# Alternating two PSUM banks in a feed-forward pass, and requesting the second-level weights two pairs ahead

## The chip, the cores and the metric

One core of a Trainium2 chip runs the whole program. The metric is the device time of one execution in microseconds. TensorE is called PE here, VectorE is DVE in the profile's rows, ScalarE ACT, GpSimd POOL; SP is the engine whose queue issues the transfers.

## The reference

A transformer block in float32 on 2048 tokens of width 1024, with modulation vectors taken from a condition `c`:

```python
h = _layernorm(x, axis=-1) * (1 + ca) + sa
x = x + ga * _A_ref(h, A_wq, A_wk, A_wv, A_wo, A_beta)   # 32 heads, 4 segments of 512 tokens with a memory
h = _layernorm(x, axis=-1) * (1 + cb) + sb
x = x + gb * _B_ref(h, B_w_gate, B_w_up, B_w_down)

def _B_ref(x, w_gate, w_up, w_down):                     # 1024 -> 3584 -> 1024
    return (_gelu(x @ w_gate) * (x @ w_up)) @ w_down
```

The change lies in the second half: the second layer norm and the gate and up products of `_B_ref`.

## The kernel before, in words

Every float32 operand is cut into a high and a low part (`cut`: ScalarE rounds the high part, VectorE or GpSimd subtracts to get the low one), and each product of a 128x128 tile is three matmuls: high x high, high x low, low x high. A matmul has 512 moving columns and fills one PSUM bank.

The program runs in stages. Attention and its projection (`project`, L753) come first; the projection works in `block(s, half)`, where s is a segment of 512 tokens. Each of the block's four tiles of 128 tokens takes 24 matmuls into a bank of a ring of two (`mm_ps`), is read out at L777 with the residual, and stored to `x1_d`. Beside it runs the second normalisation (`norm_tiles`): it loads a tile nb of `x1_d`, takes statistics (L235 to L241), scales (L246, L248), turns the tile with 8 transposes on PE (L269), applies the modulation (L275, L277) and stores to `h2_d`.

The feed-forward multiplies in Winograd's seven-product form of a 2x2 blocked product: the blocks of the left side are two token halves by two halves of the width, those of the right side are (gate, up) by the two halves of the width. Products are numbered 1 to 7. There are two groups of 1024 tokens, p = 0 and 1, and 28 chunks fc of 128 feature columns.

- The second-level stage, `two(n)` for n = 0 to 13 (L1087): products 1 and 2 of both token groups are split again in the seven-product form, over a pair of chunks. i = 1 and 2 are the two outer products. Per pair there are 14 products of 6 matmuls. The results go to `st_d`: the outer product 1 in the left half of a row, gelu of products 1 + 2 in the right half. The left sides AA stay in SBUF; `a_first` (L993) prepares them from `h2_d` while the projection ends (tiles u, cut into AA). The right sides BB of pair n + 1 are prepared beside pair n by `b_two` (L1045) from tiles g, loaded by `b_two_load` into a ring of four `raw` tiles, two to a pair. Pair 0 runs all of i = 1 and then all of i = 2; the others take turns.
- The passes, `gate_up(m)` for m = 0 to 55 (L1309): p = m // 28, and the other five products of a chunk, 12 matmuls each, go into two banks pb and pc (tiles f) out of a ring of five (`s_ps`). c1 and g1 are the two halves of the `st_d` row (`cg_load`), u2 and u3 sums in SBUF, g the pair of results that is stored to `hid_d`. In the first 28 passes `b_part(m + 1)` prepares the next chunk's weights B from `wg` and `wu` and stores them to `bc_d` and `bt_d`; in the second 28 they are read back (tiles B and ag), and `w_all` prepares the down weights beside (rw from `wd`, T, stored to `wc_d`). In the first passes `a_mix(1)` (L943) mixes the second token group (four steps, L959, whose inputs rm come by transfer), and in pass 23 `row_parts` makes the row gbb. `a_next(p)` (L1155) cuts the left sides A of a token group: twenty cuts, each into slots that the products before have left. That of group 0 runs beside pair 13, that of group 1 beside pass 27.
- The down product, `down()` (L1438), 2352 matmuls in another order of the seven.

What fixes the order: PE, VectorE, ScalarE and GpSimd run in the order in which the code is written, and from the second-level stage on SP too. Side work stands in generators on the list `sides`; `step()` (L799) advances each of them by its rate, and is called once after every product of a pair, twice per product in a pass, four times per tile of the projection. `later(k, f)` emits f k steps on; `flush` runs a side to its end.

A pass before, with the banks that the products use:

```python
product(pb, 6, True);  u2 = pb + c1            # L1335
product(pb, 7, False); u3 = pb + c1            # L1338, bank holds 6 + 7
product(pc, 5, True);  u3 = pc + u3            # L1341
product(pb, 4, False); h2 = gelu(pb + c1)      # L1346, L1347
product(pc, 3, False); u2 = pc + u2; h1 = g1 * u2; h2 = h2 * u3   # L1350 to L1352
```

Of the kernel before, what the change touches and what calls it, by code (L numbers as in the profile page):

```python
# [22 lines left out]
T = 2048  # L23
# [6 lines left out]
L = 512  # L30
# [6 lines left out]
def block_kernel(ctx: ExitStack, tc: tile.TileContext, x, c, wmod, wq, wkv, wo, beta, wg, wu, wd, out):  # L37
# [787 lines left out]
    def projections():  # L825
        def block(s, *nbs):
            for _ in project(s, [(i, nb) for i in range(4) for nb in nbs]):
                step()
                yield

        wsp = wsp_tile("xr")
        xrs.extend([[f32(wsp[:, a, b * L:(b + 1) * L]) for a in range(2) for b in range(2)], -1])
        cols = lambda s: [load_hT(oT_d, s, oh[s], f"o{s}", True), 1]
        ahead = load_hT(oT_d, 1, oh[1], "o1", True)
        sides.append([chain(islice(ahead, 1), iter([None] * 3), ahead), 1])
        two = [project(0, [(i, 0)]) for i in range(2)]
# [24 lines left out]
        ff["pools"](2)  # L861
        sides.append([ff["first"], 2])
        yield from block(3, 1)
        flush("n")
# [10 lines left out]
    PRODUCTS = (6, 7, 5, 4, 3)  # L875
# [4 lines left out]
    def feed_forward():  # L880
# [111 lines left out]

        def a_first():  # L993

            get = {1: [(raw_tile, raw_tile)] * 2, 2: [(ra_tile, ra_tile), (lambda n: pair_tile(n, "T", 5),) * 2]}
            ts = {}

            def load(i, c):
                ts[i, c] = [unit(i, c, p, get[i][c][p]) for p in range(2)]
# [3 lines left out]
            for c in range(2):  # L1003
                load(1, c)
            load(2, 0)
            for _ in range(3):
                yield
            for i in (1, 2):
                sums = {}
                if i == 2:  # L1010
                    while len(ffp) < 4:
                        yield
                    load(2, 1)
# [31 lines left out]
        def b_two(n):  # L1045
# [14 lines left out]
            yield from seven(b11, b12, b21, b22, t1, t2_, put, nc.vector, ROUND)  # L1060

        def seven(b11, b12, b21, b22, t1, t2_, put, eng, which):

            diff(t1, b12, b11)
            if 1 in which:
                put(1, b11, nc.vector)
                yield
# [5 lines left out]
            if 2 in which:  # L1073
                put(2, b21, nc.vector)
# [6 lines left out]
            put(5, t1, eng)  # L1081
# [3 lines left out]
            put(3, b22, eng)  # L1085

        def two(n):  # L1087
# [67 lines left out]
        def a_next(p):  # L1155
# [44 lines left out]
        def b_part(fc):  # L1200
# [23 lines left out]
            yield from seven(g[:, :L], u[:, :L], g[:, L:], u[:, L:], t1, t2_, put, nc.gpsimd, PRODUCTS)  # L1224
# [84 lines left out]
        def gate_up(m):  # L1309
# [23 lines left out]
            u2, u3 = (c_tile(f"c{q}_{m}") for q in range(2))  # L1333
            product(pb, 6, True)
            nc.vector.tensor_add(u2, pb, c1)  # L1335
# [5 lines left out]
            nc.vector.tensor_add(u3, pc, u3)  # L1341
            step()
            product(pb, 4, False)
            g = pair_tile(f"g{m}", "g", 3)
            h1, h2_ = (g[:, q] for q in range(2))
            nc.vector.tensor_add(h2_, pb, c1)  # L1346
            nc.scalar.activation(h2_, h2_, AF.Gelu_apprx_tanh)  # L1347
# [4 lines left out]
            nc.vector.tensor_mul(h2_, h2_, u3)  # L1352
# [194 lines left out]
        pools(3)  # L1547
        gbb = ffp[3].tile([P, D], F32, name="gbb")
        for n in range(NJ):
            if n == 1:  # L1550
                sides.append([chain(norm_tiles(x1_d, h2_d, (3,), 4, 3, "c", wait=6, get=ra_tile), wait_for(6), a_mix(0)), 1, "m"])
            if n + 1 < NJ:
                sides.append([b_two(n + 1), 1, "b"])
            else:
# [10 lines left out]
        cg_load(0)  # L1565
        for m in range(NCH):
            p, fc = divmod(m, FC)
            if m + 1 < FC:
                if m == 0:
                    gu_load(1)  # L1570
# [3 lines left out]
            if m + 1 < NCH:  # L1574
                cg_load(m + 1)
# [339 lines left out]
```

## Time and profile before

| what | us |
|---|---|
| median of 3 runs (lowest, highest) | 2900.39 (2898.39, 2905.28) |
| the profiled execution, its own time | 2895.0 |
| its span | 2893.3 |
| attention and projection | 0 to 1110 |
| second-level stage, 14 pairs | 1116 to 1450 |
| passes 0 to 27 | 1450 to 1897 |
| passes 28 to 55 | 1897 to 2356 |
| down product | 2356 to 2893 |

Times inside the trace are microseconds from the span's start. A timeline row gives start, length, engine, line, operation, output <- inputs, count, and in brackets the idle time before it with what ended it. In a view of waits a row reads: who waited <- for whom: total us, times, longest. A row by windows gives for each engine its busy time and instruction count, then the granted clock of PE (1.00 is full), the mean busy share of the 16 DMA engines and GB/s. Matmuls overlap: one takes 0.39 us from start to end, but the next starts earlier, so the end of a stretch lies later than the end of its last issue.

### The profile page before, as it was taken

The page shows a single profiled execution, that of the slowest core. Times are in us where ns is not written, and L with a number is a line of the kernel's source. Part 1 is how long each engine was busy: PE and PEld are TensorE (multiplying, and loading weights), DVE is VectorE, ACT ScalarE, POOL GpSimd, SP SyncE. Part 2 cuts the span into 40 slices and gives each one's busy share as a digit, 9 for nine tenths or more (in the row PEclk, how much of TensorE's full clock was granted, in tenths as well). Part 3 has the DMA queues.
Part 4 walks back from the last instruction along what each step waited for, and adds up shares of the span by engine and source line. Part 5 has one row for each costly group of instructions (what it writes and reads, how often), then busy time and mean ns, then how long its engine had stood idle before and what let it go on. Part 6 is the DMA issues. An engine that isn't in the chain of part 4 may idle for free.

```text
span 2893.3 us, 42626 instructions
## 1 busy us (share of the span) xinstructions
PE 2716.8 (94%) x14068; PEld 2233.6 (77%) x14068; DVE 1766.4 (61%) x3746; ACT 1260.1 (44%) x2924; POOL 1056.1 (37%) x1646
## 2 busy tenths in 40 slices
PE   7999999999999996998888999988888899999999
PEld 6888888888887885776666777767767778888887
DVE  7676658676677455666645555555656555475456
ACT  7787777766776333443422222221211233234322
POOL 3333335333335323555555666534646400000000
PEclk9999999999999998999999999989999999999999
DMA  6446446444435674565587766678988888696564
GB/s 248 134 141 164 110 126 167 118 125 130 130 114 165 213 245 132 180 210 200 195 297 280 268 245 246 230 261 304 324 298 323 301 302 273 236 308 230 174 195 140
DMA packets 266189, 613.38 MB, mean 212 GB/s; under 512 B 26992, under 2 KB 51568, under 8 KB 265968
## 3 DMA queue, kind: packets, MB, share of 16 engines
q1 hardware_dynamic: 265968, 610.66, 63.6%
q8 instruction: 111, 1.82, 0.3%
q14 instruction: 110, 0.90, 0.1%
HBM read 372.53 MB, written 187.70 MB: 194 GB/s over the span
## 4 chain that ended last, share of the span: by engine, by line
PE 73%; DVE 10%; DMA 8%; issue 4%; POOL 3%; ACT 2%; SPq 1%; DVEq 0%; POOLq 0%; ACTq 0%
PE y L1525 18%; PE f L1325 18%; PE kv L395 8%; PE q L401 6%; PE y L773 5%; PE S L607 3%; PE T L695 3%; PE O L707 3%; DMA g<-wg 2%; DVE BB L922 2%; PE kT L514 2%; PE vT L514 1%; DVE g L1352 1%; DVE c L1335 1%; PE pb L1106 1%
## 5 line engine op out<-in xcount | busy, mean ns | idle before, releaser
L1325 PE MATMUL f<-A,B 128*128 128x512 f32 x3360 | 802.3, 399 | 103.4 <-DVE c L1335 93.2
L1325 PEld LDWEIGHTS f<-A,B 128*128 128x128 f32 x3360 | 641.5, 192 | 263.8 <-DVE c L1335 63.9
L1525 PE MATMUL y<-B,L 128*128 128x512 f32 x2352 | 533.3, 389 | 0.0
L1525 PEld LDWEIGHTS y<-B,L 128*128 128x128 f32 x2352 | 441.4, 188 | 91.7
L611 ACT ACTIVATE sj<-sj,mm 128x384 f32<-128x384 f32 (+3 forms) x512 | 281.1, 552 | 40.1 <-DVE mm L609 39.5
L609 DVE CUSTOM_DVE_ANT_0 sj<-S,mask 128x384 f32<-128x384 f32 (+3 forms) x512 | 228.2, 488 | 97.8 <-PE S L607 70.8
L698 POOL TENSOR_SCALAR_AFFINE_SELECT pt<-pt 128x128 f32<-128x128 f32 x512 | 166.8, 347 | 331.1 <-ACT pt L697 323.1
L1347 ACT ACTIVATE g<-g 128x512 f32<-128x512 f32 x56 | 35.4, 632 | 514.9 <-DVE g L1346 503.5
L697 ACT ACTIVATE pt<-T 128x256 f32<-128x256 f32 (+3 forms) x512 | 182.3, 444 | 132.3 <-PE T L695 125.8
L925 ACT ACTIVATE L<-X 128x512 fp32r<-128x512 f32 x168 | 105.8, 630 | 260.0 <-PE y L1525 164.4
L922 DVE TENSOR_TENSOR L<-X,L 128x512 fp32r<-128x512 f32 x168 | 115.8, 690 | 147.7 <-ACT L L925 147.7
L386 POOL TENSOR_TENSOR w<-r,w 128x256 fp32r<-128x256 f32 x180 | 133.8, 774 | 141.7 <-ACT w L380 139.2
L1239 POOL TENSOR_TENSOR rw<-rw,gbb 128x256 f32<-128x256 f32 x112 | 103.2, 957 | 221.2 <-DMA rw<-wd 207.2
L395 PE MATMUL kv<-w,hha 128*128 128x256 f32 x896 | 175.2, 286 | 2.3 <-DVE vx L413 2.3
L1106 PE MATMUL pb<-AA,BB 128*128 128x512 f32 x504 | 132.3, 411 | 29.8 <-DVE x L1122 21.9
L395 PEld LDWEIGHTS kv<-w,hha 128*128 128x128 f32 x896 | 145.1, 192 | 3.4 <-DVE vx L413 2.5
L1106 PEld LDWEIGHTS pb<-AA,BB 128*128 128x128 f32 x504 | 97.3, 197 | 57.4 <-DVE x L1122 27.9
L395 PE MATMUL kv<-w,hla 128*128 128x256 f32 x448 | 127.3, 284 | 0.0
L773 PE MATMUL y<-wo,hho 128*128 128x512 f32 x384 | 126.5, 394 | 0.0
L925 ACT ACTIVATE B<-t 128x512 fp32r<-128x512 f32 x84 | 52.2, 621 | 147.6 <-POOL t L922 147.6
L695 PE MATMUL T<-qs,ks 128*128 128x256 f32 (+3 forms) x512 | 105.6, 327 | 1.8 <-DVE ry L674 1.1
L607 PE MATMUL S<-ks,qs 96*128 96x384 f32 (+3 forms) x512 | 106.9, 329 | 0.3
(283 smaller groups left out, 5184.5 us busy)
## 6 DMA issues: line engine op xcount, KB each, us to landing
B<-wc_d SPq DMA_DIRECT2D x112, 512.0 KB, 4.1
cg<-st_d SPq DMA_DIRECT2D x112, 256.0 KB, 5.3
hid_d<-g SPq DMA_DIRECT2D x56, 512.0 KB, 4.0
wc_d<-T SPq DMA_DIRECT2D x56, 512.0 KB, 5.3
X<-hid_d SPq DMA_DIRECT2D x112, 256.0 KB, 4.8
bc_d<-B SPq DMA_DIRECT2D x54, 512.0 KB, 5.4
B<-bc_d SPq DMA_DIRECT2D x54, 512.0 KB, 6.4
wr<-gd_d SPq DMA_DIRECT2D x84, 256.0 KB, 4.2
```

Of the source, the lines that this page charges most:

```text
L395: nc.tensor.matmul(ps, b[:, sl], w[:, a], start=(kt == 0 and a == 0 and b is hi), stop=(kt == KT - 1 and a == 1), **kw)
L401: nc.tensor.matmul(ps, w[:, a], b, start=(kt == 0 and a == 0 and b is hi), stop=(kt == KT - 1 and a == 1), **kw)
L607: nc.tensor.matmul(ps[:, :nk], qs[:96, j, i * P:(i + 1) * P], ks[:96, j, :nk], start=True, stop=True)
L609: nc.vector.tensor_tensor_reduce(out=sj[:, :nv], in0=ps[:, :nv], in1=mask[:, L - nv:], scale=-1.0, scalar=3.4e38, op0=ALU.add, op1=ALU.min ...
L611: nc.scalar.activation(sj[:, :nv], sj[:, :nv], AF.Exp, bias=mm[:, j, i:i + 1], scale=-1.0, accum_out=ll[:, i, j:j + 1])
L695: nc.tensor.matmul(ps[:, :nn], ks[:, j, kc * P:(kc + 1) * P], qs[:, j, L - nn:], start=True, stop=True)
L697: nc.scalar.activation(pt, ps[:, nn - n:nn], AF.Exp)
L773: nc.tensor.matmul(ps, b[:, i * P:(i + 1) * P], w[:, a, g % 2], start=(g == 0 and a == 0 and b is hi), stop=(g == G - 1 and a == 1))
L922: f(*xs)
L1106: nc.tensor.matmul(ps, w[:, a, at:at + P], A["a", i, r, k][b], start=(r in (1, 6, 5) and k == a == b == 0), stop=(k == 1 and a == 1), skip ...
L1325: nc.tensor.matmul(ps, B[m, i][:, a, kt * P:(kt + 1) * P], A[p, i, kt][b], start=(start and kt == 0 and a == 0 and b == 0), stop=(kt == 3 ...
L1525: nc.tensor.matmul(banks[t], ops[k][:, y, t * P:(t + 1) * P], B[slots[k]][:, x], start=(i not in (2, 4, 3) and j == 0 and x == 0 and y == ...
```

## The change

1. In a pass the products come in the order 6, 5, 7, 3, 4 (`PRODUCTS`), which puts them on the banks pb, pc, pb, pc, pb. u3 starts from product 5 and adds the bank of 6 + 7; the last multiplication of the second half is emitted two steps later. The weights for a pass are prepared in a matching order by a new function `five`, with the three differences first; `seven` keeps only the second-level stage.
2. `b_two_load(n + 2)` is called when pair n begins (before: n + 1). Pairs 1 and 2 are requested in pair 0 between its two halves, and the preparation of pair 1 begins there.
3. The first loads for the passes, `cg_load(0)`, `cg_load(1)` and `gu_load(1)`, move into pair 13, behind the last product that used the slots; `cg_load` then runs two passes ahead.
4. The normalisation of segment 2 in the projection's last blocks runs at rate 2 (before: 1).
5. In `a_first` both columns' sums are taken before the first cut, and the last tiles of i = 2 are requested as soon as their pool exists. In `a_next` the load of a further tile stands ahead of a cut instead of behind it.

```diff
-        sides.append([norm_tiles(x1_d, h2_d, (2,), 4, 3, "b", get=ff["ra"]), 1, "n"])
+        sides.append([norm_tiles(x1_d, h2_d, (2,), 4, 3, "b", get=ff["ra"]), 2, "n"])
...
-    PRODUCTS = (6, 7, 5, 4, 3)
+    PRODUCTS = (6, 5, 7, 3, 4)
...
                 for r in ROUND[1:] if i == 1 else ROUND:
-                    if (i, r) == (1, 2):
-                        continue
-                    for c in range(2):
-                        if r == 6:
+                    if r == 6:
+                        for c in range(2):
                             summed(c)
                             yield
+                    for c in range(2):
+                        if (i, r) == (1, 2):
+                            continue
...
+        def five(b11, b12, b21, b22, t1, t2_, put):
+
+            diff(t1, b12, b11)
+            yield
+            diff(t2_, b22, t1)
+            yield
+            diff(b12, b22, b12)
+            yield
+            put(6, t2_, nc.vector)
+            yield
+            put(5, t1, nc.gpsimd)
+            yield
+            put(7, b12, nc.vector)
+            diff(t2_, b21, t2_)
+            yield
+            put(3, b22, nc.gpsimd)
+            yield
+            yield
+            put(4, t2_, nc.vector)
...
                 product(i, r)
+                if n == 0 and (i, r) == (1, 3):
+                    for q in (1, 2):
+                        b_two_load(q)
+                    sides.append([chain(wait_for(1), b_two(1)), 1, "b"])
+                if n == NJ - 1 and (i, r) == (2, 4):
+                    for q in range(2):
+                        cg_load(q)
+                    gu_load(1)
                 ended(i, r)
...
             for q, (i, b) in enumerate(todo):
+                if q > 1:
+                    load()
...
                     put_a(p, i, 2 * b + k, rs[q][:, k], nc.vector)
-                    if k:
-                        load()
...
             product(pb, 6, True)
             nc.vector.tensor_add(u2, pb, c1)
             step()
+            product(pc, 5, True)
+            nc.vector.tensor_add(u3, pc, c1)
+            step()
             product(pb, 7, False)
-            nc.vector.tensor_add(u3, pb, c1)
-            step()
-            product(pc, 5, True)
-            nc.vector.tensor_add(u3, pc, u3)
-            step()
-            product(pb, 4, False)
...
+            nc.vector.tensor_add(u3, pb, u3)
             step()
             product(pc, 3, False)
             nc.vector.tensor_add(u2, pc, u2)
             nc.vector.tensor_mul(h1, g1, u2)
-            nc.vector.tensor_mul(h2_, h2_, u3)
+            step()
+            product(pb, 4, False)
+            nc.vector.tensor_add(h2_, pb, c1)
+            nc.scalar.activation(h2_, h2_, AF.Gelu_apprx_tanh)
+            later(2, lambda: nc.vector.tensor_mul(h2_, h2_, u3))
             step()
...
         pools(3)
+        units(2, 1)
...
-            if 0 < n < NJ - 1:
-                b_two_load(n + 1) if n + 1 not in two_raws else None
-            if n == NJ - 2:
+            if 0 < n < NJ - 2:
+                b_two_load(n + 2)
+            elif n == NJ - 2:
                 gu_load(0)
...
-            if m + 1 < NCH:
-                cg_load(m + 1)
+            if m + 2 < NCH:
+                cg_load(m + 2)
```

More of the change, by code (lines that the diff above doesn't have):

```diff
@@ L991, in a_early, with units @@
                     yield
+        get = {1: [(raw_tile, raw_tile)] * 2, 2: [(ra_tile, ra_tile), (lambda n: pair_tile(n, "T", 5),) * 2]}
+        ts = {}
+        def units(i, c):
+            ts[i, c] = [unit(i, c, p, get[i][c][p]) for p in range(2)]
         def a_first():
[L995 to L999, printed above, removed]
             while not normed(0, 2):
@@ L1003, in a_first @@
             for c in range(2):
-                load(1, c)
-            load(2, 0)
+                units(1, c)
+            units(2, 0)
             for _ in range(3):
@@ L1009, in a_first @@
                 sums = {}
[L1010 to L1013, printed above, removed]
+                while (i, 1) not in ts:
+                    yield
                 def summed(c):
@@ L1059, in b_two, with seven @@
             t1, t2_ = (tmp_tile(f"t{q}_a{n}").rearrange("p (i m) -> p i m", i=2) for q in (1, 2))
-            yield from seven(b11, b12, b21, b22, t1, t2_, put, nc.vector, ROUND)
-        def seven(b11, b12, b21, b22, t1, t2_, put, eng, which):
+            yield from seven(b11, b12, b21, b22, t1, t2_, put)
+        def seven(b11, b12, b21, b22, t1, t2_, put):
             diff(t1, b12, b11)
-            if 1 in which:
-                put(1, b11, nc.vector)
-                yield
+            put(1, b11, nc.vector)
+            yield
             diff(t2_, b22, t1)
@@ L1072, in seven @@
             yield
-            if 2 in which:
-                put(2, b21, nc.vector)
+            put(2, b21, nc.vector)
             diff(b12, b22, b12)
@@ L1080, in seven @@
             yield
-            put(5, t1, eng)
+            put(5, t1, nc.vector)
             yield
@@ L1084, in seven @@
             yield
-            put(3, b22, eng)
+            put(3, b22, nc.vector)
+        def five(b11, b12, b21, b22, t1, t2_, put):
[13 more added lines that the diff above has]
+            put(3, b22, nc.gpsimd)
+            yield
+            yield
+            put(4, t2_, nc.vector)
         def two(n):
@@ L1223, in b_part @@
                 t1, t2_ = (a_tile(48 + 2 * (fc % 2) + q, f"t{q}_{fc}", F32) for q in range(2))
-            yield from seven(g[:, :L], u[:, :L], g[:, L:], u[:, L:], t1, t2_, put, nc.gpsimd, PRODUCTS)
+            yield from five(g[:, :L], u[:, :L], g[:, L:], u[:, L:], t1, t2_, put)
         def w_all():
@@ L1333, in gate_up @@
             u2, u3 = (c_tile(f"c{q}_{m}") for q in range(2))
+            g = pair_tile(f"g{m}", "g", 3)
+            h1, h2_ = (g[:, q] for q in range(2))
             product(pb, 6, True)
@@ L1551, in feed_forward @@
                 sides.append([chain(norm_tiles(x1_d, h2_d, (3,), 4, 3, "c", wait=6, get=ra_tile), wait_for(6), a_mix(0)), 1, "m"])
-            if n + 1 < NJ:
+            if 0 < n < NJ - 1:
                 sides.append([b_two(n + 1), 1, "b"])
-            else:
+            elif n:
                 flush("m")
@@ L1564, in feed_forward @@
             flush("b")
-        cg_load(0)
         for m in range(NCH):
```

6 lines of the change are left out of this document (removed).

## The prediction

> **What bounds the kernel now.** I read the page first. Its chain that ended last is 73% PE, and among its groups these three carry the argument (busy us and mean ns of one, then idle time before them and its releaser):
>
> ```profile
> PE 73%; DVE 10%; DMA 8%; issue 4%; POOL 3%; ACT 2%; SPq 1%; DVEq 0%; POOLq 0%; ACTq 0%
> ...
> L1325 PE MATMUL f<-A,B 128*128 128x512 f32 x3360 | 802.3, 399 | 103.4 <-DVE c L1335 93.2
> ...
> L1525 PE MATMUL y<-B,L 128*128 128x512 f32 x2352 | 533.3, 389 | 0.0
> ```
>
> The last row gives PE's own pace, since nothing interrupts it: 533.3 / 2352 = 0.2267 us for a 128x512 matmul. A product of a pass (12 matmuls) is then 2.72 us, a pass (60) 13.60, 28 passes 380.9, a pair of the second-level stage (84) 19.05. The passes' 3360 matmuls would take 761.8 us; they are busy for 802.3 and stand idle for 103.4 more. Who ends PE's waits, from the view of waits, and then the stretches of the feed-forward (length; busy time and count of PE, PEld, DVE, ACT, POOL; clock; DMA share; GB/s): first pair, pair 1, pairs 2 to 12, pair 13, first 28 passes, second 28, down product.
>
> ```profile
> PE f L1325 <- DVE c L1335: 93.2, 56, 7.0
> ...
> PE pa L1106 <- ACT c L1116: 9.3, 8, 2.7
> PE f L1325 <- DVE c L1341: 9.1, 4, 2.8
> ...
> PE pa L1106 <- DVE xr L777: 6.2, 1, 6.2
> ```
> ```profile
> 1116.45:1160.62 44.17, 27.54 (x84) 20.57 (x85) 29.38 (x40) 15.91 (x27) 19.55 (x21) 0.74 0.33 113
> 1160.62:1180.02 19.40, 19.40 (x90) 16.07 (x88) 12.56 (x22) 10.14 (x17) 11.96 (x16) 1.00 0.32 109
> 1180.02:1418.90 238.88, 219.79 (x955) 174.40 (x954) 154.58 (x247) 96.90 (x173) 127.32 (x157) 1.00 0.60 201
> 1418.90:1450.27 31.37, 25.75 (x86) 19.02 (x85) 19.70 (x32) 16.50 (x30) 13.60 (x18) 0.78 0.66 214
> 1450.27:1897.40 447.13, 400.96 (x1697) 320.29 (x1695) 249.62 (x315) 108.77 (x188) 268.38 (x328) 0.98 0.74 263
> 1897.40:2356.36 458.96, 401.76 (x1670) 321.86 (x1669) 260.80 (x341) 92.15 (x172) 202.57 (x224) 0.96 0.84 299
> 2356.36:2893.30 536.94, 533.28 (x2353) 441.25 (x2351) 298.77 (x465) 170.63 (x284) 0.00 (x0) 1.00 0.68 229
> ```
>
> Against PE's pace the stretches lose 25.1, 0.3, about 27, 12.3, 66.2, 78.1 and 3.6 us. The change works on all but the last. 56 waits on L1335 are one in every pass: product 7 adds onto the bank in which product 6 has just ended, and VectorE must first read it out.
>
> **The passes, first 28.** The timeline of PE shows the quiet ones as stretches of 60 matmuls, each opened by that wait:
>
> ```profile
> 1640.68 13.88 PE L1325 MATMUL f<-A,B 128*128 128x512 f32 x60 [0.95 <-DVE c L1335]
> 1655.52 13.88 PE L1325 MATMUL f<-A,B 128*128 128x512 f32 x60 [0.95 <-DVE c L1335]
> ```
>
> A pass is 14.84 us, 1.24 above 13.60: 0.95 of idle and the 0.28 by which a new stretch's last matmul ends late (13.88). The change puts product 5, on the other bank, between 6 and 7, and so on through the pass. VectorE's queue in pass 10, before (c0 is u2, c1 is u3, f0 and f1 are the two banks, B11 weights for the next pass):
>
> ```order
> L1335 TENSOR_TENSOR c0_10_18633<-f0_10_18631,cg10_0_18514 128x512
> L922 TENSOR_TENSOR B11_6_18663<-t1_11_18644,B11_6_18663 128x512
> L1338 TENSOR_TENSOR c1_10_18634<-f0_10_18631,cg10_0_18514 128x512
> L922 TENSOR_TENSOR B11_7_18681<-ru11_18511,B11_7_18681 128x512
> L1341 TENSOR_TENSOR c1_10_18634<-f1_10_18632,c1_10_18634 128x512
> L1346 TENSOR_TENSOR g10_18709<-f0_10_18631,cg10_0_18514 128x512
> ```
>
> And the same place after:
>
> ```order
> L1362 TENSOR_TENSOR c0_10_18636<-f0_10_18634,cg10_0_18399 128x512
> L1365 TENSOR_TENSOR c1_10_18637<-f1_10_18635,cg10_0_18399 128x512
> L922 TENSOR_TENSOR B11_6_18677<-t1_11_18647,B11_6_18677 128x512
> L1368 TENSOR_TENSOR c1_10_18637<-f0_10_18634,c1_10_18637 128x512
> L922 TENSOR_TENSOR B11_7_18697<-ru11_18514,B11_7_18697 128x512
> L1371 TENSOR_TENSOR c0_10_18636<-f1_10_18635,c0_10_18636 128x512
> L1372 TENSOR_TENSOR g10_18638<-cg10_1_18400,c0_10_18636 128x512
> L922 TENSOR_TENSOR B11_4_18727<-t1_11_18647,B11_4_18727 128x512
> L1375 TENSOR_TENSOR g10_18638<-f0_10_18634,cg10_0_18399 128x512
> ```
>
> The banks alternate f0, f1, f0, f1, f0, so each read now has a whole product, 2.72 us, before PE needs the bank; it cost PE 1.24 with no cover. The seven VectorE operations of a pass stay seven. They need 249.62 / 28 = 8.9 us a pass with everything else on VectorE, and GpSimd 268.38 / 28 = 9.6, both below 13.60. So a quiet pass should be 13.60.
>
> What the cover does not hide is a VectorE that stands for more than 2.72 us behind another wait. The four steps of the second mixing do that (L959; the read-out L1341 queues behind it):
>
> ```profile
> 1487.41 0.69 DVE L959 TENSOR_TENSOR m<-rm,rm 128x512 f32<-128x512 f32 x1 [4.76 <-DMA rm<-h_d]
> 1488.02 0.68 DVE L1341 TENSOR_TENSOR c<-f,c 128x512 f32<-128x512 f32 x1
> ```
>
> L1341 already has one product of cover and still lost 9.1 us in 4 times; I keep 6. The first pass loses 6.96 us because its cg tile is requested only at the end of pair 13:
>
> ```profile
> 1459.32 0.69 DVE L1335 TENSOR_TENSOR c<-f,cg 128x512 f32<-128x512 f32 x1 [4.15 <-DMA cg<-st_d]
> ...
> 1460.15 7.41 PE L1325 MATMUL f<-A,B 128*128 128x512 f32 x24 [6.96 <-DVE c L1335]
> ```
>
> The change loads two passes' cg tiles and the weights of pass 1 inside pair 13, after the last product on those slots, so this wait goes; I leave 4 us for entry, the gbb row and the change of A tiles. Sum: 380.9 + 6 + 4 = 391 for 447.1, a gain of **56** (45 if a third of the 66.2 stays, 62 at most).
>
> **The passes, second 28.** Here VectorE's read comes late by its own queue in every other pass: 3.58 us of PE waiting, with L1335 behind three operations of 1.2 us.
>
> ```profile
> 2101.22 13.91 PE L1325 MATMUL f<-A,B 128*128 128x512 f32 x60 [0.78 <-DVE c L1335]
> 2118.72 15.52 PE L1325 MATMUL f<-A,B 128*128 128x512 f32 x60 [3.58 <-DVE c L1335]
> ```
> ```profile
> 2114.58 1.22 DVE L1352 TENSOR_TENSOR g<-g,c 128x512 f32<-128x512 f32 x1
> 2115.73 1.21 DVE L922 TENSOR_TENSOR B<-ag,B 128x512 fp32r<-128x512 f32 x1
> 2116.86 1.21 DVE L922 TENSOR_TENSOR T<-rw,T 128x512 fp32r<-128x512 f32 x1
> 2117.98 0.68 DVE L1335 TENSOR_TENSOR c<-f,cg 128x512 f32<-128x512 f32 x1
> ```
>
> With 2.72 us of cover under 1 us of that is left, and the 1.6 us by which such a pass runs long afterwards (15.52 for 13.91) goes too. But the transfers then come near their end. This stretch moves 299 GB/s x 459.0 us = 137 MB. The fullest 25 us of it, from the view by windows:
>
> ```profile
> 2200.00:2225.00 25.00, 22.45 (x97) 18.24 (x98) 14.36 (x20) 2.72 (x5) 14.72 (x16) 1.00 0.98 358
> ```
>
> At a share of 0.98 it carries 358 GB/s; 137 MB at that rate are 383 us, just above PE's 380.9, and the traffic is thinner at both ends, so the middle is bound by it. I take 14.4 us a pass for the 24 passes with the down weights' preparation, 13.6 for four, and 3 at the start, 403 for 459.0: a gain of **56**. It lies between 0 (only the present rate) and 75 (no limit). The Trainium skill, DMA: Bandwidth & Descriptors, section Where 436 GB/s comes from, says that HBM to SBUF transfers are bound at about 358 GB/s per core; its section Measured gives 425 GB/s for one core alone. The row agrees with the first; by the second this stretch would take PE's 381 us and gain 75.
>
> **The second-level stage.** Weights for pair n+1 are now requested when pair n begins and used at once. GpSimd and ScalarE stop for them, and c of the half that PE waits for queues behind on ScalarE:
>
> ```profile
> POOL t_a L922 <- DMA g<-wg: 51.5, 11, 6.5
> ```
> ```profile
> 1273.18 0.63 ACT L925 ACTIVATE BB<-g 128x512 fp32r<-128x512 f32 x1 [4.29 <-DMA g<-wg]
> 1273.72 0.58 ACT L1116 ACTIVATE c<-pa 128x512 f32<-128x512 f32 x1
> ```
>
> Pairs 2 to 12 lose 238.9 - 11 x 19.05 - 2.5 (transposes) = 27 us. That it can go is seen in pair 1, whose weights were there: 19.40 us, all busy. The new load waits on SP for the cuts of the previous pair, with the st_d stores behind it; these have no reader for many pairs. I take **20** (12 to 27).
>
> Pair 13 has twenty A cuts on VectorE besides its own work in both versions: **1** (0 to 8).
>
> **Normalisation and first pair.** At twice the rate the four tiles' transposes stand 12 matmuls (2.72 us) apart on PE instead of 24. VectorE's queue before, in the projection's last block (nb tiles of segment 2, y a projection tile's bank):
>
> ```order
> L240 TENSOR_SCALAR rsb1024_14377<-mvb1024_14373 128x1
> L246 TENSOR_SCALAR mrb1024_14394<-mvb1024_14373,rsb1024_14377 128x1
> L777 TENSOR_TENSOR xr_12821<-y3_0_1_14365,xr_12821 128x512
> L235 BN_STATS stb1152_14413<-nb1152_14380 128x6 x2
> L238 BN_AGGR mvb1152_14414<-stb1152_14413 128x2
> ```
>
> And after:
>
> ```order
> L240 TENSOR_SCALAR rsb1024_14357<-mvb1024_14353 128x1
> L777 TENSOR_TENSOR xr_12821<-y3_0_0_14319,xr_12821 128x512
> L922 TENSOR_TENSOR AA1_2_1_1_14371<-u1_1_0_14295,AA1_2_1_0_14370 128x512
> L246 TENSOR_SCALAR mrb1024_14374<-mvb1024_14353,rsb1024_14357 128x1
> L235 BN_STATS stb1152_14385<-nb1152_14360 128x6 x2
> ```
>
> The second tile's statistics moved ahead by one projection tile (5.44 us), and L246 now stands behind a bank that PE has not finished. Statistics to scaled tile take VectorE, GpSimd and ScalarE in turn, so PE will wait at each tile's transposes where now it does not:
>
> ```profile
> 1069.68 1.28 DVE L235 BATCH_NORM_STATS2 stb<-nb 128x6 f32<-128x512 f32 x2
> ...
> 1072.06 0.21 DVE L246 TENSOR_SCALAR mrb<-mvb,rsb 128x1 f32<-128x1 f32 x1 [0.66 <-POOL rsb L241]
> ...
> 1072.36 1.24 ACT L248 ACTIVATE nb<-nb,mrb,rsb 128x1024 f32<-128x1024 f32 x1 [16.43 <-issue]
> ```
>
> From 1069.68 to 1073.60 the chain takes 3.92 us against 2.72: each tile is at least 1.2 late, more where the queue's other reads stand in it. I take 1.5, 6 in all. In return segment 2 is stored some 8 steps earlier, the cuts for the first pair leave the end of the projection, and the 6.2 us on L777 go: these two cancel. What is left is the first pair: 25.1 us lost, of which the second half's tiles, now requested ahead, return a third. I take **8** (0 to 18).
>
> **The sum.** 56 + 56 + 20 + 1 + 8 = 141 from the profiled execution's own 2895.0 (span 2893.3 and 1.7 around it): 2754. The median of the runs shown, 2900.4, stands 5.4 above that execution, so I predict 2759.
>
> **The rivals.**
> Transfers have room: the second stretch is PE's, 384 for 459, 75 instead of 56, so 2740. For it, the mean share of the stretch is 0.84, so there is some slack; against it, the share of 0.98 at 358. The Trainium skill's 425 GB/s on the page named above would lead here. 0.2.
> Transfers stay at the present rate: higher latency stops GpSimd and ScalarE, and VectorE behind them; the second stretch keeps 459: 141 - 56 = 85, 2815. For it, one queue issues every transfer in order, and 0.84 is already high for that. 0.2.
> The change does not do what it says: VectorE reads the bank as late as PE needs it, behind cuts that wait for ScalarE, and the 93.2 + 9.1 stay under a new line, less the first pass's 7: 141 - 95 - 10 (clock and restart) = 36, 2864. Against it, the 0.95 of the quiet passes, which is the read alone. 0.07.
> Slower: the saturated queue makes every pass of the second stretch start as one does now, when VectorE was late at the change of A tiles:
>
> ```profile
> 1902.09 16.41 PE L1325 MATMUL f<-A,B 128*128 128x512 f32 x60 [4.66 <-DVE c L1335]
> ```
>
> That is 21.07 us a pass, 590 for 459: 131 lost against 85 gained, 2946. It decides against the change from 544 / 28 = 19.4 us a pass; the fullest window still ran PE for 22.45 of 25 us. 0.03.
>
> **How the numbers follow.** The forecast has 0.5. The range 2725 to 2815 takes in both transfer rivals and, with the first of them, most of the open ends of the pairs (2710 if every term is at its best); outside lie the last two rivals and the best corner. About 0.2% (5.8 us) is what a measurement of this kernel can tell from no change: slower 0.03, within 0.01, faster 0.96.
>
> **What would show it.** PE's waits on the first read-out fall from 93.2 to under 15 with quiet passes of 13.6; pairs 2 to 12 near 219; transposes of nb wait a few us; the second 28 passes last about 403 at 340 GB/s. Wrong is: passes of the first stretch above 14.3 (then the bank was not it), or a second stretch above 430 at the same GB/s.

## The result, and the profile after

| what | before | after |
|---|---|---|
| median of the runs, us (lowest, highest) | 2900.29 (2898.39, 2905.28) | 2744.03 (2738.30, 2744.98) |
| ratio, with its 95% interval | | 0.9455 (0.9437 to 0.9472) |
| the profiled execution, its span | 2893.3 | 2742.3 |

The kernel became 156 us faster, 15 more than the 141 forecast; 2744 lies inside the range of 2725 to 2815. It came out where the first rival had put it (2740: the transfers have room).

The page of after. The passes' matmuls have almost lost their idle time (before: 103.4 us), and the down product is what it was:

```profile
L1350 PE MATMUL f<-A,B 128*128 128x512 f32 x3360 | 766.0, 391 | 8.9 <-ACT B L925 3.8
L1550 PE MATMUL y<-B,L 128*128 128x512 f32 x2352 | 533.9, 390 | 0.6 <-DVE L L922 0.3
```

Of PE's waits (who waited <- for whom: total us, times, longest) the passes keep four kinds, of which the first read-out, now L1362, has 2.9 us in three where it had 93.2 in 56. The normalisation's transposes wait four times, and the 6.2 us on the projection's last read-out are gone:

```profile
PE pb L1123 <- DVE x L1139: 15.4, 6, 5.6
...
PE tpb L269 <- ACT nb L248: 6.0, 4, 1.6
...
PE f L1350 <- ACT B L925: 3.8, 1, 3.8
PE f L1350 <- DVE c L1362: 2.9, 3, 2.2
...
PE f L1350 <- ACT y L1156: 1.2, 1, 1.2
...
PE f L1350 <- DVE c L1368: 0.9, 1, 0.9
```

The stretches of after, in the order of the prediction's: first pair, pair 1, pairs 2 to 12, pair 13, first 28 passes, second 28, down product.

```profile
1121.43:1160.38 38.95, 26.69 (x85) 20.58 (x84) 21.81 (x32) 13.19 (x23) 13.18 (x15) 0.78 0.36 122
1160.38:1183.27 22.89, 20.26 (x86) 15.42 (x85) 15.95 (x23) 10.93 (x20) 15.48 (x19) 1.00 0.42 138
1183.27:1397.95 214.68, 213.86 (x958) 176.56 (x956) 154.32 (x249) 98.88 (x175) 128.42 (x157) 1.00 0.65 218
1397.95:1428.83 30.88, 23.29 (x86) 17.27 (x84) 20.16 (x30) 16.21 (x30) 15.20 (x18) 0.89 0.68 220
1428.83:1819.60 390.77, 384.78 (x1685) 317.13 (x1684) 238.52 (x314) 104.34 (x185) 273.72 (x328) 1.00 0.86 298
1819.60:2204.18 384.58, 381.69 (x1681) 315.31 (x1680) 258.53 (x345) 95.83 (x173) 205.62 (x224) 1.00 0.97 358
2204.18:2742.30 538.12, 533.86 (x2353) 441.45 (x2351) 297.74 (x463) 171.33 (x285) 0.00 (x0) 1.00 0.68 230
```

One correction to the stretches of before. Counted by matmuls (60 to a pass), its pass 28 begins at 1894.60; the prediction's boundary, 1897.40, lay 2.8 us too late. By the count the first 28 passes took 444.3 and the second 461.8:

```profile
1450.27:1894.60 444.33, 398.16 (x1686) 318.27 (x1685) 246.82 (x311) 105.97 (x183) 268.38 (x328) 0.98 0.74 262
1894.60:2356.36 461.76, 404.56 (x1682) 323.87 (x1680) 263.60 (x345) 94.95 (x177) 202.57 (x224) 0.96 0.84 300
```

| stretch | forecast, us less | found | how |
|---|---|---|---|
| first 28 passes | 56 | 53.5 | 444.3 to 390.8 |
| second 28 passes | 56 | 77.2 | 461.8 to 384.6 |
| pairs 2 to 12 | 20 | 24.2 | 238.9 to 214.7 |
| pair 13 | 1 | 0.5 | 31.4 to 30.9 |
| projection and first pair | 8 | 4.2 | first projection matmul to pair 1: 253.7 to 249.5 |
| pair 1 | no term | -3.5 | 19.4 to 22.9 |
| down product | 0 | -1.2 | 536.9 to 538.1 |
| all that stands ahead of the projection | 0 | -4.0 | starts at 910.9, before 906.9 |
| sum | 141 | 150.9 | the spans differ by 151.0 |

The last row but one is no effect of the change: the program is the same up to there, and in the twelve kernels tried below the first projection matmul starts anywhere between 906.8 and 912.2. The rest of the 156 is the 5.3 us by which the profiled run of before lay under its median; after's lies on it.

PE's timeline shows what became of the second 28 passes: three waits in 385 us, and between them stretches of 480, 540 and 636 matmuls (8, 9 and 10.6 passes) at PE's own pace.

```profile
1827.44 109.08 PE L1350 MATMUL f<-A,B 128*128 128x512 f32 x480 [2.23 <-DVE c L1362]
1936.86 122.70 PE L1350 MATMUL f<-A,B 128*128 128x512 f32 x540 [0.33 <-DVE c L1362]
2059.89 144.46 PE L1350 MATMUL f<-A,B 128*128 128x512 f32 x636 [0.33 <-DVE c L1362]
```

The stretch moves 358 GB/s x 384.6 us = 138 MB, the same bytes as before, but not with 358 as an upper end. By windows of 25 us, a full one of after stands beside one of before (the start of its down product):

```profile
1975.00:2000.00 25.00, 25.00 (x112) 20.71 (x111) 16.70 (x24) 5.50 (x10) 15.84 (x17) 1.00 1.02 396
```
```profile
2350.00:2375.00 25.00, 25.00 (x112) 20.70 (x111) 14.61 (x23) 10.00 (x19) 0.00 (x0) 1.00 1.02 358
```

Both have a DMA share of 1.02, one at 396 GB/s and one at 358. The share is no gauge of what is left.

### The profile page after: what moved, and what is told of

It is laid out like the page before. It is cut to its first block, busy times and chain, and to the rows that moved or that the text cites. A ratio compares the mean times of both kernels' runs of the same rounds, so it can differ in the third digit from the quotient of the medians.

```text
span 2742.3 us, 42592 instructions
## 1 busy us (share of the span) xinstructions
PE 2677.0 (98%) x14068; PEld 2227.6 (81%) x14068; DVE 1753.4 (64%) x3746; ACT 1261.3 (46%) x2924; POOL 1066.2 (39%) x1646
## 4 chain that ended last, share of the span: by engine, by line
PE 52%; DMA 3%; DVE 3%; POOL 1%; issue 1%; ACT 1%; SPq 0%; DVEq 0%; POOLq 0%; ACTq 0%
PE f L1350 25%; PE y L1550 19%; PE pb L1123 3%; PE pc L1123 2%; PE pa L1123 2%; DMA rm<-h_d 1%; DVE A L922 1%; DMA ra<-mix_d 1%; DMA X<-hid_d 0%; DMA u<-h_d 0%; DMA wr<-gd_d 0%; POOL y L922 0%; DMA ru<-wu 0%; DVE AA L922 0%; DMA mix_d<-rm 0%
## 5 line engine op out<-in xcount | busy, mean ns | idle before, releaser
L1350 PE MATMUL f<-A,B 128*128 128x512 f32 x3360 | 766.0, 391 | 8.9 <-ACT B L925 3.8
L1350 PEld LDWEIGHTS f<-A,B 128*128 128x128 f32 x3360 | 631.7, 188 | 142.8 <-ACT B L925 6.8
L1376 ACT ACTIVATE g<-g 128x512 f32<-128x512 f32 x56 | 35.4, 633 | 415.7 <-DVE g L1375 402.1
L1264 POOL TENSOR_TENSOR rw<-rw,gbb 128x256 f32<-128x256 f32 x112 | 109.2, 1009 | 155.9 <-DMA rw<-wd 150.6
```

Source lines behind the costliest of these rows:

```text
L1350: nc.tensor.matmul(ps, B[m, i][:, a, kt * P:(kt + 1) * P], A[p, i, kt][b], start=(start and kt == 0 and a == 0 and b == 0), stop=(kt == 3 ...
```

## Experiments: where the gain comes from

In the rows of an experiment the line numbers differ from after's by a few. Theory: the bank turn gains in both halves of the passes, up to PE's pace; the early weights gain in the pairs; nothing else matters much. Rivals stand in each expectation.

**The bank turn alone**, on the kernel before:

```diff
-    PRODUCTS = (6, 7, 5, 4, 3)
+    PRODUCTS = (6, 5, 7, 3, 4)
+        def five(b11, b12, b21, b22, t1, t2_, put):
...
             product(pb, 6, True)
             nc.vector.tensor_add(u2, pb, c1)
             step()
+            product(pc, 5, True)
+            nc.vector.tensor_add(u3, pc, c1)
+            step()
             product(pb, 7, False)
...
```

> The kernel before with the bank turn alone: the order 6, 5, 7, 3, 4, the weights of a pass in that order, nothing else. Theory (the turn frees PE in both halves of the passes, and the second 28 passes end at PE's pace, not at the transfers'): first 28 passes 447 to about 398 (the first pass keeps its 7 us wait for its cg tile), second 28 from 459 to about 385, rest unchanged, together some 123 less: about 2778 by the median. Rival 1 (the earlier loads carry part of the passes' gain): 2800 or more, with waits for cg in the passes. Rival 2 (the terms as predicted, the transfers binding the second half when they are not also loaded further ahead): second half about 403, 2796.

Measured 2775.13 beside 2902.11 of before on the same chip, ratio 0.9563 (0.9540 to 0.9587): 127 less. The waits on the first read-out, the passes 2 to 27, and the second 28:

```profile
PE f L1345 <- DVE c L1357: 7.4, 4, 4.3
```
```profile
1494.29:1849.67 355.38, 355.38 (x1565) 293.55 (x1564) 217.17 (x286) 95.19 (x169) 245.75 (x294) 1.00 0.85 290
1849.67:2235.79 386.12, 383.11 (x1680) 316.04 (x1679) 257.56 (x345) 95.89 (x173) 206.59 (x224) 1.00 0.97 358
```

The turn by itself brings the passes to where after has them (by the count of matmuls 355.4 and 384.6); both rivals fall. The order in which the weights are prepared (`five`) moves with the turn, in this run and in the next; what the two are worth apart was not measured.

**All but the bank turn**: the changed kernel with the old order put back.

```diff
-    PRODUCTS = (6, 5, 7, 3, 4)
+    PRODUCTS = (6, 7, 5, 4, 3)
...
             step()
+            product(pb, 7, False)
+            nc.vector.tensor_add(u3, pb, c1)
+            step()
             product(pc, 5, True)
-            nc.vector.tensor_add(u3, pc, c1)
+            nc.vector.tensor_add(u3, pc, u3)
             step()
...
```

> The changed kernel with the old order of a pass (6, 7, 5, 4, 3 and its weights' order) put back: everything but the bank turn. Theory: only the second-level stage (24 less in pairs 2 to 12, 4 less up to the end of the first pair, 3.5 more in pair 1) and the first pass (7 less) gain: some 32 less, about 2868 by the median, with quiet passes at 14.84 again and about 93 us of waits on the first read-out less the first pass's 7. Rival (the turn needs nothing and the loads ahead carry half of the passes' gain): 2830 or less.

Measured 2873.48 (0.9901, 0.9875 to 0.9927): 28.6 less than before; with the 127.0 of the turn alone that makes 155.6, and the whole change gave 156.3. The two parts add up. PE's wait, then pairs 2 to 12 and the second 28 passes:

```profile
PE f L1355 <- DVE c L1365: 90.8, 56, 5.7
```
```profile
1179.64:1393.57 213.93, 213.32 (x955) 176.07 (x954) 153.46 (x249) 98.55 (x174) 128.95 (x157) 1.00 0.65 219
...
1868.64:2329.71 461.07, 405.45 (x1682) 324.54 (x1681) 262.23 (x345) 95.02 (x177) 206.86 (x224) 0.96 0.84 299
```

The pairs have their gain and the passes have none (before: 461.8 at 300 GB/s).

**Weights one pair ahead again**, pair 1's not requested inside pair 0:

```diff
-            if 0 < n < NJ - 2:
-                b_two_load(n + 2)
+            if 0 < n < NJ - 1:
+                b_two_load(n + 1) if n + 1 not in two_raws else None
...
-                if n == 0 and (i, r) == (1, 3):
-                    for q in (1, 2):
-                        b_two_load(q)
-                    sides.append([chain(wait_for(1), b_two(1)), 1, "b"])
```

> The changed kernel with the second-level weights requested one pair ahead again and pair 1's not requested inside pair 0. Theory (the wait of GpSimd and ScalarE for the weights g cost the pairs 2 to 12 their 24 us): pairs 2 to 12 back from 215 to about 239 and the 3.5 us of pair 1 gone, 2764 by the median. Rival (the pairs gained from other edits or from a run's variation): under 2754, pairs 2 to 12 at 225 or less.

Measured 2766.19 (0.9531, 0.9504 to 0.9558). GpSimd waits for the weights again, pair 1 is all busy again, and pairs 2 to 12 are long again:

```profile
POOL t_a L922 <- DMA g<-wg: 54.6, 11, 7.4
```
```profile
1159.26:1178.67 19.41, 19.41 (x89) 16.12 (x88) 12.79 (x23) 10.14 (x17) 11.75 (x15) 1.00 0.31 109
1178.67:1422.24 243.57, 223.99 (x955) 177.99 (x954) 155.13 (x248) 97.12 (x173) 127.06 (x158) 0.98 0.59 197
```

**Normalisation at rate 1 again:**

```diff
-        sides.append([norm_tiles(x1_d, h2_d, (2,), 4, 3, "b", get=ff["ra"]), 2, "n"])
+        sides.append([norm_tiles(x1_d, h2_d, (2,), 4, 3, "b", get=ff["ra"]), 1, "n"])
```

> The changed kernel with the normalisation of segment 2 at rate 1 again. Theory (the prediction's: the four waits of 1.5 us at the transposes and the 6.2 us at the projection's last read-out cancel): 2744 within 3 us, with the waits on nb at 0 and the wait on L777 back at about 6. Rival 1 (the rate brings the 5 us by which the first pair is shorter): 2749. Rival 2 (the rate only costs its 6 us, the gain in the first pair is that of the earlier sums and tiles): 2738.

Measured 2745.83 (0.9461, 0.9437 to 0.9484), not to be told from after. The four waits on nb are gone and the old one is back:

```profile
PE pa L1123 <- DVE xr L777: 6.1, 1, 6.1
```

From the first projection matmul to pair 1 it takes 251.4 (908.4 to 1159.8), after 249.5; the eight kernels that are alike up to there take 248.1 to 250.3. So the rate is worth about 2 us, 6.0 paid and 8 got back. That the other half of the 4.2 belongs to the earlier sums and tiles follows by difference; no run takes those out.

**The passes' first loads put back** (cg one pass ahead, none in pair 13):

```diff
-                if n == NJ - 1 and (i, r) == (2, 4):
-                    for q in range(2):
-                        cg_load(q)
-                    gu_load(1)
...
+        cg_load(0)
         for m in range(NCH):
...
-            if m + 2 < NCH:
-                cg_load(m + 2)
+            if m + 1 < NCH:
+                cg_load(m + 1)
```

> The changed kernel with the passes' loads back where they were: cg one pass ahead and its first one after pair 13, weights of pass 1 at pass 0. The prediction's step: the first pass waited 6.96 us for its cg tile and loses that wait; then passes 0 and 1 go from 35.3 to about 42 us here and the whole from 2744 to about 2751, all later passes unchanged. Rival (pass 0 and 1 wait for the cuts of weights B on GpSimd and ScalarE in any case, which hides the cg tile): 35 to 37 for the two, 2745. A second rival: cg one pass ahead comes late in the full second half: waits on L1362 in most passes, second 28 passes over 395.

Measured 2748.28 (0.9472, 0.9444 to 0.9500). Passes 0 and 1 take 38.5 (23.2 + 15.3) against 35.4 (after: 1428.83 to 1464.24 by the count of matmuls; 35.1 to 36.9 in the five kernels that are alike up to there); all others are as in after. On PE's timeline of this run the wait for the cg tile is back, but the one for the cuts of B behind it shrinks from 3.83 to 0.48:

```profile
1440.69 8.33 PE L1346 MATMUL f<-A,B 128*128 128x512 f32 x24 [5.97 <-DVE c L1358]
1449.50 13.88 PE L1346 MATMUL f<-A,B 128*128 128x512 f32 x60 [0.48 <-ACT B L925]
```

The two waits overlap, so the early loads are worth 2 to 3 us and not 7: between theory and rival. Two passes ahead brings nothing later on.

## Experiments: where the transfers end

The prediction held the second 28 passes to 403 us, because the fullest window of before stood at 358 GB/s and a share of 0.98. After runs them in 384.6. Where is the end?

**Two spare reads a pass** in 23 of the second 28 passes, into cg slots that stand empty:

```diff
+            def spare(x):
+                if FC < m < NCH - 4:
+                    for q in range(2):
+                        t = a_tile(40 + 2 * ((m + 3) % 4) + q, f"sp{m}_{q}_{x}", F32)
+                        nc.sync.dma_start(t, wu[fc][:, q * L:(q + 1) * L])
...
             product(pc, 5, True)
+            spare(1)
             nc.vector.tensor_add(u3, pc, c1)
```

> The changed kernel with two spare reads of 256 KB in each of 23 passes of the second half (into cg slots that stand empty), which nothing uses: 12.1 MB on top of 137.7. The prediction's step (transfers bind at 358 GB/s): 149.7 MB need 418 us, second 28 passes 384.6 to about 418, 2777. Theory now (the stretch is bound by PE, and the transfers' limit lies above the 396 GB/s of its fullest 25 us): 385 to 388, 2744 to 2748, with the fullest windows near 410 GB/s. Between them (a limit at 396): the 23 passes need 410, so some 11 us more, 2755.

Measured 2741.61 (0.9454, 0.9428 to 0.9481), as after. The second 28 passes, and 70 us of their middle (1990 to 2060) in forty slices of GB/s:

```profile
1815.28:2198.57 383.29, 381.06 (x1681) 315.24 (x1680) 252.52 (x345) 98.03 (x173) 195.58 (x224) 1.00 1.01 391
```
```profile
GB/s 411 423 412 418 406 405 413 411 413 419 414 412 417 412 407 420 414 413 418 407 406 405 419 406 423 414 405 417 416 412 405 418 418 419 411 414 418 407 408 412
```

391 GB/s on average, and PE with one gap, of 2.2 us at the start: 358 is no bound. The slices lie between 405 and 423; in after the same view goes from 266 to 424. A rate that no longer varies is what a ceiling looks like, at about 413.

**Four spare reads a pass:**

```diff
             nc.vector.tensor_add(u3, pb, u3)
             step()
+            spare(3)
```

> The same with four spare reads in each of those passes: 24.1 MB on top, 161.8 in all. At a limit of 358 GB/s: 452, 2811. At 396: the 23 passes need 449 GB/s, 313 us become 355, so 427 and 2786. No limit below 449: 385 to 390, 2745 to 2750. Whichever comes, the rate of the fullest windows is the transfers' real end for this mix.

Measured 2814.45 (0.9701, 0.9670 to 0.9732), within 4 us of what a limit of 358 GB/s gives, at a mean of 352:

```profile
1817.72:2276.84 459.12, 405.55 (x1682) 323.76 (x1680) 243.57 (x345) 101.46 (x173) 180.38 (x224) 0.96 0.96 352
```

Taken alone this run would have confirmed the prediction's bound. But the rate fell below that of the run with fewer bytes, which a ceiling alone does not explain, and the second read into each slot must wait for the first on SP's queue.

**Four spare reads of half the size** (as many issues and waits as four, as many bytes as two, in pieces of 1 KB where the others have 2 KB):

```diff
-                        nc.sync.dma_start(t, wu[fc][:, q * L:(q + 1) * L])
+                        nc.sync.dma_start(t[:, :L // 2], wu[fc][:, q * L:q * L + L // 2])
```

> The kernel with four spare reads a pass, each cut to half its size (128 KB): as many issues and the same waits of the issuing queue for a slot's earlier read as with four whole ones, but the 12.1 MB of the two whole ones. Theory (the 74 us that four whole reads cost are the transfers' ceiling, about 413 GB/s by the run with two): the stretch stays PE's, 384 to 390, 2742 to 2750. Rival (they are the issuing queue standing behind the second read into a slot, 91 us of its waits, with the loads of B and ag behind it): most of the 74 stays, over 430 and over 2790.

Measured 2795.49 (0.9638, 0.9617 to 0.9658): the outcome of the rival. The second 28 passes of this run, then what SP's queue and ScalarE wait for in 1850 to 2200:

```profile
1819.30:2256.26 436.96, 401.15 (x1682) 321.46 (x1680) 239.96 (x345) 101.33 (x173) 182.98 (x224) 0.97 0.95 343
```
```profile
SPq L1361 <- DMA sp<-wu: 88.1, 21, 6.0
```
```profile
ACT B L925 <- DMA ag<-bt_d: 149.7, 33, 6.9
```

With the same bytes as the run that lost nothing, 52 of the 75 us are there. SP stands behind the second read into a slot, the loads of B and ag behind it are issued late, ScalarE waits for ag, VectorE behind it reads the banks late, and PE stops. This is the chain of the second rival (transfers that come late), set off by the order on the issuing queue and not by a rate. In the run with two whole reads no wait of SP's queue for an earlier transfer lasts over 1.6 us, and ScalarE's wait for ag is 75.3 us in 30. It was not separated how much of the 52 are these waits, how much the greater number of issues and how much the smaller pieces. But the next run adds as many issues, 92, and twice the bytes, with no wait of SP's queue for a transfer over 1.5 us, and loses 25.5 us against the run with two reads: if the copies cost an issue no less than a read does, the issues alone are at most half of it.

**Two spare reads and two copies** from DRAM to DRAM, with no second transfer into any slot:

```diff
                         nc.sync.dma_start(t, wu[fc][:, q * L:(q + 1) * L])
+                        nc.sync.dma_start(sp_d[(fc * 2 + q) * P:(fc * 2 + q + 1) * P], wu[fc][:, q * L:(q + 1) * L])
```

> The kernel with two spare reads a pass and, behind each, a copy of 256 KB from one place of DRAM to another that nothing has used and nothing waits for: 12.1 MB of reads and 12.1 MB of copies on top of 137.7 in 23 passes, with no second transfer into a slot. Theory (the run with two reads alone already stood at the transfers' ceiling, 413 GB/s in the full windows): the 23 passes need 449 GB/s, 313 us become about 340, the second 28 passes 384 to about 411 at 395 GB/s, 2770. Rival 1 (the ceiling is higher still, 413 was only what was asked for): 384 to 390, windows near 450, 2745. Rival 2 (a copy costs twice, once for each of its ends): some 40 more than the theory, 2810.

Measured 2766.56 (0.9522, 0.9501 to 0.9543). The second 28 passes, and one of their windows:

```profile
1820.45:2229.28 408.83, 390.18 (x1681) 315.85 (x1680) 248.61 (x345) 101.35 (x173) 183.73 (x224) 0.99 1.01 395
...
2025.00:2050.00 25.00, 23.48 (x103) 18.81 (x102) 13.78 (x21) 6.46 (x11) 9.41 (x13) 1.00 1.04 412
```

408.8 at 395 GB/s, where 411 at 395 was expected, and no 25 us above 414; both rivals fall. The ceiling for this mix is 410 to 414 GB/s, and after asks for 370 in the middle of the stretch (1850 to 2175). Every transfer here goes out through SP's one queue, which from 1850 to 2200 waits for earlier transfers for 174 us in this run and 162 with two reads, against 26 in after. Whether the ceiling is that of the transfers or that of one queue was not separated.

## Experiments: what is left

**The weights of pass 1 requested when pair 13 begins.** On GpSimd's timeline of after the differences for pass 1 begin late, and the cuts behind them stop PE for 3.83 us in pass 0:

```profile
1439.75 1.43 POOL L922 TENSOR_TENSOR t<-ru,rg 128x256 f32<-128x256 f32 x2 [3.35 <-DMA ru<-wu]
```

```diff
             elif n == NJ - 2:
                 gu_load(0)
+            if n == NJ - 1:
+                gu_load(1)
             two(n)
```

> The changed kernel with the weights of pass 1 requested when pair 13 begins, not after its last product but three. Theory (GpSimd's differences for pass 1 wait 3.35 us for ru, and the cuts behind them stop PE for 1.2 + 3.8 us in passes 0 and 1): these waits go, passes 0 and 1 from 35.3 to about 29, 2738. Rival (the six A loads of pair 13 stand behind the 2 MB and the cuts of A come later): pair 13 longer by 3 or more, 2744 to 2748.

Measured 2743.05 (0.9456, 0.9431 to 0.9482), no difference. Pair 13, then passes 0 and 1:

```profile
1395.84:1427.99 32.15, 24.27 (x84) 17.89 (x83) 19.22 (x29) 15.98 (x30) 14.52 (x18) 0.84 0.74 243
1427.99:1443.97 15.98, 14.05 (x61) 11.05 (x60) 10.34 (x15) 5.35 (x9) 10.99 (x14) 1.00 1.00 363
1443.97:1460.61 16.64, 13.88 (x62) 11.16 (x61) 9.87 (x12) 4.20 (x7) 15.41 (x20) 1.00 1.01 369
```

Passes 0 and 1 give 2.7 (32.7 for 35.4), pair 13 takes 1.3 of it: half theory, half rival. Of the two waits that the theory names, the 3.83 falls to 0.16, but the 1.2 stays, as 1.77: there VectorE comes late to the first read-out, behind the read-outs and cuts of pair 13. And PE's wait on L1368 in pass 1 grows from 0.93 to 2.76.

**Three edits together**, on that kernel: pair 1's preparation begins with pair 0, and one more tile lets six A loads go out ahead.

```diff
-                    for q in (1, 2):
-                        b_two_load(q)
-                    sides.append([chain(wait_for(1), b_two(1)), 1, "b"])
+                    b_two_load(2)
...
-            if 0 < n < NJ - 1:
+            if n < NJ - 1:
                 sides.append([b_two(n + 1), 1, "b"])
...
-            for _ in range(5):
+            for _ in range(6 if p == 0 else 5):
                 load()
```

> The changed kernel with three edits where it still loses: the preparation of pair 1 begins with pair 0 again (only pair 2's weights are requested inside pair 0), the weights of pass 1 are requested when pair 13 begins, and six of the ten A loads of the first token group have a tile from the start (one more in the ring g). Theory: pair 1 from 23.2 to 19.4 with pair 0 one longer, pair 13 from 31 to 28 or less, passes 0 and 1 at 32.5 or less: 6 to 9 us, 2736. Rival (GpSimd, VectorE and the loads of these stretches only hand the wait on): 2741 to 2744.

Measured 2740.25 (0.9446, 0.9426 to 0.9466; after: 0.9437 to 0.9472). Pair 1 takes 19.4 again, with pair 0 at 40.0 (after 39.0), and passes 0 and 1 by the count of matmuls 34.4 (35.4); pair 13 stays at 32.6 (30.9). From pair 0 to pass 1 that is 1.8 us less; the intervals do not tell it from after.

**Six late cuts of A on GpSimd**, on top:

```diff
-                    put_a(p, i, 2 * b + k, rs[q][:, k], nc.vector)
+                    put_a(p, i, 2 * b + k, rs[q][:, k], nc.gpsimd if p == 0 and 5 <= q < 8 else nc.vector)
```

> The same with the low parts of six late cuts of A on GpSimd, which stands idle for 8 to 9 us in pair 13. Theory (VectorE's queue, with read-outs behind cuts that wait for transfers, is what pair 13 loses its 12 us to): pair 13 at 25 or less, 2 to 4 us below the run without it. Rival (GpSimd's own late work, the differences for pass 1, then starts late): passes 0 and 1 longer by as much, no gain.

Measured 2745.40 (0.9467, 0.9446 to 0.9489), 5 us more than the run without it, on the same chip. Pair 13 falls to 29.5, but passes 0 and 1 take 37.1 (34.4), while passes 2 to 27 take 355.4 in both: the outcome of the rival. Its cause is only half seen: the differences for pass 1 begin 12.4 us after pass 0, 7.8 without the edit, but PE's own waits there (2.8 and 3.4 us) are on VectorE. No version here beats the changed kernel beyond doubt.

## Why the prediction was right, and where it was off

**The bank turn.** Right in mechanism and in size for the first 28 passes: 391 forecast, 390.8 found, and the experiment with the turn alone shows that it carries the passes by itself. Together the two halves have 94.5 us less idle time of PE (103.4 to 8.9) and 36.3 less busy time (802.3 to 766.0): a wait also cost PE its late restart (the 0.28 of the prediction's rows), and the granted clock, 0.98 and 0.96 in the two halves before, is 1.00 after.

The two small terms inside, 6 and 4, came to 9.9, but by luck: they were off in opposite directions. Of the 6 us for the second mixing PE sees 0.9, once, in pass 1:

```profile
1459.47 1.18 DVE L959 TENSOR_TENSOR m<-rm,rm 128x512 f32<-128x512 f32 x1 [2.97 <-DMA rm<-h_d]
```
```profile
1461.40 178.90 PE L1350 MATMUL f<-A,B 128*128 128x512 f32 x788 [0.93 <-DVE c L1368]
```

The cover of 2.72 us alone does not explain it, since L1341 had one too and lost 9.1. What changed is VectorE's wait for rm: four of 4.4 to 5.4 us before, and 3.0, 1.0, 0.8 and 1.4 after, of which only the first is longer than the cover. It goes with the turn (4.1, 1.0, 1.4 and 0.9 with the turn alone, 4.2 to 5.4 without it); why VectorE then waits less was not found out. The 4 us for entry are 8.2, the 0.9 among them: passes 0 and 1 take 35.4 for 27.2. There the step "this wait goes" was too simple, since behind the cg tile stood the cuts of B with a wait of nearly the same end.

**The second 28 passes** are the step that failed: "the middle is bound by" 358 GB/s, 403 us. The mechanism on PE was right, the bound was not there. 358 was the highest rate that before had asked for in a full window, at a share of 0.98, and a highest value that was seen is not a ceiling. The term is 77, not 56, and the stretch is PE's. Of the two figures of the Trainium skill that the prediction weighed (DMA: Bandwidth & Descriptors), the one in the section Where 436 GB/s comes from, 358 GB/s per core, disagrees with the 391 that the run with two spare reads sustained; the 425 in its section Measured, given for one core alone (with about 358 for each of two that stream at once), is near the 410 to 414 found here. The rival with room for the transfers deserved the larger chance.

**The pairs.** Right: 20 forecast, 24 found, all of it the weights (25 to 29 come back in the two kernels that request them late). That pair 1, forecast at nothing, pays 3.5 us was overlooked: the preparation for it begins in the middle of pair 0 and runs on into it, where read-outs queue behind its cuts. With the preparation from the start of pair 0 it is 19.4.

**Normalisation and first pair.** The four waits came to 6.0 in all, as worked out, and the 6.2 on L777 went; the net was 4.2 and not 8. Pair 13 was 0.5 for 1.

**The median.** The 5.4 us from the profiled execution to the median of before were carried over to after, whose profiled execution lies on its median.

Of the 15 us by which the forecast was too high, the transfers make 21, the median 5 and the pairs 4; the smaller misses (pair 1, the run's first 900 us, the first pair, the first passes, the down product, pair 13) take back 15.

## What to carry to other kernels

Where a product adds onto a bank that has just been read out, another product on a second bank between the two hides the whole read-out; here that was worth 127 us, for waits of 93 us in 56 passes and the slow restarts behind them. The rate in the fullest window of a profile is a lower bound of what the transfers can do: before it is taken for the end, add traffic that nothing waits for, and see whether the slices of the rate turn flat. When such a test is made, its transfers must wait for nothing on the issuing queue, or it measures the queue.

## What the runs showed of the hardware

- Through one issuing queue, one core moved 391 GB/s over 383 us with PE at its own pace, and 410 to 414 GB/s at most over 25 us in any mix tried, with the DMA share at 1.03 to 1.04. A share of 0.98 to 1.02 was seen at rates from 352 to 396 GB/s.
- 8.8% more bytes (12.1 on 137.7 MB) cost nothing, and a further 8.8% cost 25.5 us, 6.7%. The same first 8.8% in half-size reads, with waits of 88 us on the issuing queue, cost 52 us.
- The program's first 900 us vary by 5 us between the profiled runs of fourteen kernels that are alike up to there, more than most of the small terms here.
